# Keeping VectorE's and GpSimd's products apart in the planned order of a fused attention and MLP kernel, and giving GpSimd fewer of them

## The chip, the cores and the metric

The kernel runs on one core of a Trainium2 chip. The metric is the time of one execution on the device in microseconds, less is better. A core has five engines that each work through a fixed list of instructions: TensorE (PE, with its weight loads shown as PEld), VectorE (DVE), ScalarE (ACT), GpSimd (POOL) and SyncE (SP), which issues transfers. They wait for each other by semaphores.

## The reference, cut to what matters

Cosine attention over 8 batches of 12 heads, 448 tokens and 64 columns a head, and then a token-mixing and channel MLP with residuals on what the attention gives.

```
q_n = q / (norm(q) + 1e-6);  k_n = k / (norm(k) + 1e-6)     # unit vectors
attn = softmax(q_n @ k_n.T / tau);  a = attn @ v            # [8, 12, 448, 64]
x = a as [8, 448, 768]
u = x + (x.T @ U @ V).T                                     # U [448, 32], V [32, 448]
out = u + relu(u @ w_ch1) @ w_ch2                           # 768 -> 3072 -> 768
```

## The kernel before

**The work.** Each batch's queries and keys come in three loads of four heads (`load_qk`, L588, issued by GpSimd). For each load `stats` makes the scale of every vector: a square of half a load (`squares`: L636 on ScalarE, L638 on GpSimd or L640 on VectorE), a sum over the head's columns (L644, VectorE), a logarithm and an exponential for the root (L658 and L659, ScalarE), and the inverse (L664 and L666, VectorE). `norm` then makes the unit vectors, for each pair of heads two products with the inverse (L712): part 0 is the queries, part 1 the keys. In batches 0 and 1 the result is transposed by TensorE (L566) and copied by ScalarE or VectorE (L1436, L1438); from batch 2 on SyncE transposes it by a transfer (L728).

The scores of a pair (L774) go to PSUM, ScalarE takes their exponential (L787 and L792), TensorE multiplies by the values (L819), and VectorE divides by the row's sum: L855 and L857 in batches 0 and 1, L850 and L851 later. The division frees the PSUM bank of L819. Token mixing is L934 and L987 on TensorE, and L996 and L998 add its result on VectorE. The MLP works on tiles of 128 tokens of two batches at a time: first three tiles and then one in the plain form (L1372 up, L1414 down, L1425 adds and stores), then twelve pairs of tiles in a Strassen form with seven products instead of eight. The first seven of these use it for the second matrix only (L1260 up, L1289 down), the last five for both (L1153 up). Their sums are L1175, L1232 to L1234, L1243 and L1307 on VectorE and L1314 on GpSimd. `seven_rows` (L1112 to L1115) prepares weights for the last five in buffers that the attention has left.

**The order.** The kernel holds its own planner. Each piece of work is an `Op` with an engine, an assumed duration, what it depends on, what buffers it takes and gives back, and a priority. `Plan.run` plays the work through in assumed time and writes each engine's list in the order in which the play started it. On the chip only this order and the semaphores of the dependencies hold; assumed times do not. TensorE and GpSimd have several streams of work with a fixed order in each; ScalarE, VectorE and SyncE take what is ready by priority. Work that may go to ScalarE or VectorE is decided in the play, too.

An `Op` may be marked `port`. In the play, a marked operation on VectorE does not start while a marked one runs on GpSimd, and the other way round (`shared` in `Plan.run`); nothing on the chip comes from the mark:

```
def shared(o, e, r):
    return max(r, port["POOL" if e == "DVE" else "DVE"]) if o.port and e in port else r
```

The squares and the MLP's weight and sum operations are marked. Of the unit vectors, only those that GpSimd makes are. Which these are stands in `POOL_XN`: part 0 in batches 2 to 7, six products in each batch. GpSimd also makes the four squares of the third load of batch 0. Where the play finds TensorE idle in the first batch, warm-up matmuls (L698) are put in, by the length of the hole.

Of the kernel before, what the change touches and what calls it, by code (L numbers as in the profile page):

```python
# [317 lines left out]
def kernel(  # L318
# [14 lines left out]
    B, H, S, D = q.shape  # L333
# [14 lines left out]
    BURST = [1] + [2] + [3] * 6  # L348
    PLAIN = [3, 1]
    HALF = 7  # L350
    POOL_XN = {x: (0,) for x in range(2, B)}
    WHOLE = 3
    LAST = {0: 0, 2: 2, 4: 4}, {0: 0, 2: 0, 4: 4}
    WIDE = 1
# [69 lines left out]
    class First:  # L424

        slot = uv
# [72 lines left out]
    plan = Plan()  # L499
# [12 lines left out]
    pool_x = plan.stream("POOL")  # L512
# [9 lines left out]
    def dve_t(n, fast=1, fixed=0.065):  # L522
        return fixed + n * 0.00105 / fast

    def any_t(n, fast=1, fixed=0.065):
        return {"ACT": act_t(n), "DVE": dve_t(n, fast, fixed)}
# [27 lines left out]
    def flip(stream, ins, n, into, part, deps, acq, rel, wide=1, eng="ACT/DVE", took=0.05):  # L554


        tp = Slot(r_mm, 1)
        tp.own = True
        for z, x in enumerate(ins):
            def fn(z=z, x=x):  # L560
                if z == 0:
                    w = len(ins) // wide
                    tp.tile = bank_t[:, tp.group[0], :].bitcast(BF)[:, 0:w * n].rearrange(
                        "p (w n) -> p w n", w=w)
                m = 128 // wide
                nc.tensor.transpose(out=tp.tile[m * (z % wide):m * (z % wide + 1), z // wide, :], in_=x(),  # L566
                                    identity=ident[:n, :n])
            o = plan.add(Op("PE", took, fn, deps=deps + [id_set] if z == 0 else (), acq=[tp] + acq,
                            rel=rel if z == len(ins) - 1 else []), stream)
        took = any_t(n * len(ins) // wide, 2)  # L570
        c = plan.add(Op(eng, took, None, deps=[o], acq=acq, rel=[tp], prio=0.2, fast=True))

        def move():
            for dst, src in part(into(), tp.tile):
                copy_op(c, dst, src)
        c.fn = move
        return c
# [45 lines left out]
    def squares(b, g, ld, ops, lo, ii, ss, pr, on, hold, then):  # L623

        red = []
        for i in ii:
            for a0 in range(0, g, G // 2):
                a1 = min(g, a0 + G // 2)
                sq = Slot(r_sq, 1)
                o = Op(on, 1.3 if on == "POOL" else 0.48 if on == "ACT" else 0.44, None,  # L630
                       deps=[ops[i], *hold], acq=[sq], prio=pr + 0.2, fast=True, port=True)

                def square(o=o, i=i, a0=a0, a1=a1, sq=sq):
                    x, y = ld.tile[:, i, lo + a0:lo + a1, :], sq.tile[:, 0:a1 - a0, :]
                    if o.by == "ACT":
                        nc.scalar.activation(out=y, in_=x, func=AF.Square)  # L636
                    elif o.by == "POOL":
                        nc.gpsimd.tensor_mul(y, x, x)  # L638
                    else:
                        nc.vector.tensor_mul(y, x, x)  # L640
                o.fn = square
                plan.add(o, pool_q if on == "POOL" else None)
                red.append(plan.add(Op("DVE", dve_t(256 * (a1 - a0)),
                    lambda i=i, a0=a0, a1=a1, sq=sq: nc.vector.reduce_sum(  # L644
                        ss.tile[:, i, a0:a1, :].rearrange("p h c -> p (h c)"),
                        sq.tile[:, 0:a1 - a0, :].rearrange("p h (c d) -> p (h c) d", d=D),
                        axis=AX.X),
                    deps=[o, *then], acq=[ss], rel=[sq], prio=pr + 0.1)))
        return red
# [50 lines left out]
    def norm(b, p, ld, la, inv, a, deps, pr, loaded):  # L700


        by_pe = b < PE_BATCHES
        first = b == 0 and p == 0
        xn, qkT = Slot(r_xn, 2 if by_pe and (first or (b, p) not in RAW_KEYS) else 1), Slot(r_qkT, SC if b == 0 else sum(p in members(b, x) for x in groups_of(b)))

        def part(i):
            def fn():
                src = ld.tile[:, i, la:la + 2, :].rearrange("p h (c d) -> p h c d", d=D)
                sc = inv.tile[:, i, a:a + 2, :].unsqueeze(3).to_broadcast([SCH, 2, SC, D])  # L710
                dst = xn.tile[:, SC * (1 - i):SC * (2 - i), :].rearrange("p c (h d) -> p h c d", h=2)
                (nc.gpsimd if pool_ else nc.vector).tensor_mul(dst, src, sc)  # L712
            pool_ = i in POOL_XN.get(b, ())
            return plan.add(Op("POOL" if pool_ else "DVE", 1.2 if pool_ else dve_t(512), fn, deps=[deps[i]], acq=[xn],
                               rel=[getattr(ld, "slot", ld), inv], prio=pr, port=pool_), pool_x if pool_ else None)

        def raw():
            c = Op("ACT/DVE", any_t(512), None, deps=loaded[1], acq=[xn], rel=[ld.slot], prio=-0.9)
            c.fn = lambda: copy_op(
                c, xn.tile[:, 0:SC, :].rearrange("p c (h d) -> p h c d", h=2),  # L720
                ld.tile[:, 1, la:la + 2, :].rearrange("p h (c d) -> p h c d", d=D))
            return plan.add(c)

        keys = (b, p) in RAW_KEYS
        ops = {0: part(0), 1: raw()} if first and keys else {0: part(0)} if keys else {
            i: part(i) for i in ((0, 1) if first else (1, 0))}
        if not by_pe:
            done = [plan.add(Op("SP", 0.1, lambda: nc.sync.dma_start_transpose(  # L728
                out=qkT.tile, in_=xn.tile.rearrange("p b e -> p (b e)")), deps=list(ops.values()), acq=[qkT],
                rel=[xn], prio=0, lat=("x", 0.05 * 56, 5.0)))]  # L730
        else:
            done = []
            for i in (1, 0) if keys else ops:
                b0, b1 = SC * (1 - i), SC * (2 - i)
                ins = [(lambda z=z: xn.tile[:, z, :]) for z in range(b0, b1)] if i in ops else [
                    (lambda c=c, hh=hh: ld.tile[:, 1, la + hh, D * c:D * c + D]) for c in range(SC) for hh in range(2)]
                done.append(flip(
                    pe_tp, ins, SCH,
                    lambda: qkT.tile, (lambda t_, x, b0=b0, b1=b1: [(t_[:, b0:b1, :], x)]),
                    [ops[i]] if i in ops else loaded[1], [qkT], [xn if i in ops else ld], len(ins) // SC,  # L740
                    "ACT/DVE", 0.05))
        got[b, p, "qkT"] = (qkT, done, (inv, a, deps[1]))
        return list(ops.values())
# [4 lines left out]
    def members(b, slots):  # L748
        return sorted({p for p, _ in slots} | {p + 1 for p, c in slots if b >= WIDE and c == SC - 1})
# [684 lines left out]
    def copy_op(op, dst, src):  # L1434
        if op.by == "ACT":
            nc.scalar.copy(out=dst, in_=src)  # L1436
        else:
            nc.vector.tensor_copy(out=dst, in_=src)  # L1438
# [52 lines left out]
    def groups_of(b):  # L1491
        if b < WIDE:
            slots = [(p, c) for p in range(NPAIR) for c in range(SC)]
            return [slots[n:n + BURST[b]] for n in range(0, len(slots), BURST[b])]
        slots = []
        for p in range(NPAIR):
            if b >= TB:
                slots += [(x, SC - 1) for x, at in LAST[b > TB].items() if at == p]
            slots += [(p, c) for c in range(SC - 1)] + ([(p - 1, SC - 1)] if p % 2 and b < TB else [])
        return [sorted(slots[n:n + BURST[b]], key=lambda x: x[1] == SC - 1) for n in range(0, len(slots), BURST[b])]  # L1500
# [6 lines left out]
    def att(b):  # L1507
# [18 lines left out]
        acq=[uv], prio=-5, lat=2.5)) for i, src in enumerate((q, k))]  # L1526
# [8 lines left out]
    for c in range(SC):  # L1535
# [8 lines left out]
                        deps=[zf, *begun], prio=-2, lat=12.0))]  # L1544
# [104 lines left out]
```

## Time and profile before

| | |
|---|---|
| median of three runs | 553.93 us (553.42 to 554.13) |
| the profiled execution | 553.89 us, its span 552.1 us |
| TensorE clock granted, mean | 0.997 |
| busy: PE, DVE, ACT, POOL | 542.2, 435.1, 281.4, 184.0 us |
| L712 on DVE, batches 0 to 7 | 58 products, shortest 628 ns, median 682 ns, longest 1532 ns |
| L712 on POOL, batches 2 to 7 | 36 products, shortest 1034 ns, median 1044 ns, longest 1551 ns |
| warm-up matmuls | 142, the last at 31.0 us |
| last exponential of batch 0 ends | 36.86 us |

The profile is of one execution. Busy times of TensorE overlap in its pipeline, so a busy share near 100% does not by itself say that it works at its peak. A line such as L712 can run on two engines and then has two groups. Times within the execution are counted from the start of the span.

### The profile page before, as it was taken

To read this page: it belongs to the slowest core of one execution; us is meant where nothing else is said; L and a number is where in the kernel's file an instruction comes from. 1 tells how busy PE (TensorE), PEld (TensorE's weight loads), DVE (VectorE), ACT (ScalarE), POOL (GpSimd) and SP (SyncE) were. 2 spreads that over 40 slices of the span, in tenths; PEclk is the share of its full clock that TensorE was granted. 3 is DMA by queue.
4 is the path that set the end of the run, shared out by engine and by line. 5 is a ranking of instruction groups with operands and counts; after the bars stand their busy time and mean duration, and the time that the engine had idled before them with its cause. 6 is when DMAs were issued, how large, how long until landed. Compare 5 with 4: busy or idle time off the path is not lost.

```text
span 552.1 us, 14798 instructions
## 1 busy us (share of the span) xinstructions
PE 542.2 (98%) x6085; PEld 390.2 (71%) x6086; DVE 435.1 (79%) x978; ACT 281.4 (51%) x458; POOL 184.0 (33%) x216
## 2 busy tenths in 40 slices
PE   8899999999999999999999999999999999999996
PEld 6565565577857857767767767767778787878784
DVE  8889969989978897798789859657658585858583
ACT  7875746475575656656745754743314141414140
POOL 8626235325533552851543381020101111111111
PEclk9899999999999999999999999999999999999999
DMA  9999999959586949977997494332231312121201
GB/s 147 200 206 144 204 204 148 205 96 139 75 175 108 136 80 172 118 121 160 100 159 135 73 147 102 71 59 60 63 87 31 87 30 87 32 86 30 87 4 57
DMA packets 142324, 61.08 MB, mean 111 GB/s; under 512 B 101008, under 2 KB 142256, under 8 KB 142256
## 3 DMA queue, kind: packets, MB, share of 16 engines
q0 software_dynamic: 72352, 25.73, 43.0%
q1 hardware_dynamic: 69904, 34.41, 29.0%
q8 instruction: 47, 0.77, 0.6%
q14 instruction: 21, 0.17, 0.1%
HBM read 56.93 MB, written 15.93 MB: 132 GB/s over the span
## 4 chain that ended last, share of the span: by engine, by line
PE 91%; DVE 6%; ACT 1%; issue 1%; DMA 1%; DVEq 0%
PE bank L1289 30%; PE bank L1260 20%; PE bank L1153 13%; PE bank L819 8%; PE bank L774 7%; PE bank L1372 6%; PE bank L1414 4%; DVE qk_all L712 2%; PE bank L987 1%; DVE ss L644 1%; ACT attn L787 1%; PE bank L566 1%; PE bank L934 1%; DVE X_sb L857 1%; DMA relu<-in_q_dram 1%
## 5 line engine op out<-in xcount | busy, mean ns | idle before, releaser
L792 ACT ACTIVATE attn<-bank 128x896 bf16<-128x896 f32 (+1 forms) x163 | 140.4, 916 | 44.3 <-PE bank L774 43.8
L1289 PEld LDWEIGHTS <-relu 128*128 128x128 bf16 x1008 | 95.7, 98 | 66.4 <-issue 7.1
L1260 PE MATMUL bank<-uT,w_sb 128*128 128x256 bf16 x1008 | 120.2, 273 | 0.0
L1260 PEld LDWEIGHTS <-w_sb 128*128 128x128 bf16 x1008 | 95.2, 98 | 20.0 <-issue 7.9
L1289 PE MATMUL bank<-w_sb,relu 128*128 128x384 bf16 x576 | 102.7, 326 | 0.0
L712 POOL TENSOR_TENSOR qk_all<-qk_all,inv 112x512 bf16<-112x512 bf16 x36 | 41.0, 1148 | 85.0 <-DMA sqk<-qk_all 39.0
L644 DVE TENSOR_REDUCE ss<-sqk 112x8 f32<-112x512 bf16 x96 | 62.5, 672 | 4.4 <-ACT sqk L636 4.1
L819 PEld LDWEIGHTS <-attn 128*128 128x128 bf16 (+1 forms) x1536 | 55.1, 98 | 7.7 <-issue 4.2
L819 PE MATMUL bank<-v_nat,attn 128*128 128x65 bf16 (+1 forms) x1536 | 58.1, 194 | 0.9 <-DVE X_sb L857 0.4
L1270 ACT ACTIVATE relu<-bank 128x512 bf16<-128x512 f32 x53 | 31.6, 597 | 44.0 <-PE bank L1260 43.8
L774 PE MATMUL bank<-sqk 64*128 64x448 bf16 (+1 forms) x384 | 48.8, 359 | 1.1 <-ACT sqk L1436 0.5
L636 ACT ACTIVATE sqk<-qk_all 112x512 bf16<-112x512 bf16 x56 | 33.8, 632 | 23.3 <-DVE ss L644 22.0
L712 DVE TENSOR_TENSOR qk_all<-qk_all,inv 112x512 bf16<-112x512 bf16 x57 | 45.4, 821 | 0.3
L1153 PEld LDWEIGHTS <-w_sb 128*128 128x128 bf16 x720 | 41.0, 98 | 0.6
L1314 POOL TENSOR_TENSOR relu<-relu,u_nat 128x384 f32<-128x384 f32 x8 | 9.5, 1182 | 91.4 <-ACT relu L1312 91.3
L1190 ACT COPY attn<-bank 128x512 f32<-128x512 f32 x15 | 8.8, 585 | 60.4 <-PE bank L1153 59.5
L611 POOL DMA_DIRECT2D v_nat<-in_v_dram x42 | 31.2, 748 | 15.1 <-DMA w_sb<-in_moe_w_ch_dram 11.8
L1372 PE MATMUL bank<-uT,w_sb 128*128 128x384 bf16 (+1 forms) x288 | 35.6, 273 | 0.0
L1414 PE MATMUL bank<-w_sb,relu 128*128 128x384 bf16 x192 | 35.3, 326 | 0.0
L851 DVE TENSOR_TENSOR X_sb<-bank,rd 128x256 bf16<-128x256 f32 x72 | 30.5, 424 | 2.5
L1307 DVE TENSOR_TENSOR O_sb<-bank,O_sb 128x384 f32<-128x384 f32 x35 | 19.2, 554 | 16.2 <-PE bank L1289 11.5
L1153 PE MATMUL bank<-uT,w_sb 128*128 128x128 bf16 x540 | 31.8, 219 | 0.0
(137 smaller groups left out, 820.0 us busy)
## 6 DMA issues: line engine op xcount, KB each, us to landing
qk_all<-in_q_dram POOLq DMA_DIRECT2D x23, 224.0 KB, 4.4
qk_all<-in_k_dram POOLq DMA_DIRECT2D x23, 224.0 KB, 6.5
u_nat<-u SPq DMA_DIRECT2D x25, 192.0 KB, 2.8
w_sb<-in_moe_w_ch_dram POOLq DMA_DIRECT2D x4, 1152.0 KB, 17.7
w_sb<-in_moe_w_ch_dram POOLq DMA_DIRECT2D x8, 576.0 KB, 15.8
u<-X_sb SPq DMA_DIRECT2D x22, 192.0 KB, 4.7
v_nat<-in_v_dram POOLq DMA_DIRECT2D x11, 168.0 KB, 7.8
out_dram<-O_sb SPq DMA_DIRECT2D x12, 144.0 KB, 2.1
```

Of the source, the lines that this page charges most:

```text
L636: nc.scalar.activation(out=y, in_=x, func=AF.Square)
L644: lambda i=i, a0=a0, a1=a1, sq=sq: nc.vector.reduce_sum(ss.tile[:, i, a0:a1, :].rearrange("p h c -> p (h c)"), sq.tile[:, 0:a1 - a0, :].re ...
L712: (nc.gpsimd if pool_ else nc.vector).tensor_mul(dst, src, sc)
L774: nc.tensor.matmul(out=out, lhsT=qkT.tile.rearrange("p b s -> p (b s)")[r, n0:n0 + w], rhs=qkT.tile[r, SC:2 * SC, :].rearrange("p c s -> p ...
L792: exps.append(plan.add(Op("ACT", act_t(2 * S, 0.08), lambda sc=sc, c=c, attn=attn: nc.scalar.activation(out=attn.tile[:, :, off:off + S] i ...
L819: nc.tensor.matmul(out=av.tile[:, t, 0:D + 1], lhsT=tail.tile[:, hh, 128 * t:128 * (t + 1)] if tail and j == SC - 1 else (attn if j < SC - ...
L1153: o = plan.add(Op("PE", pe_t(128), lambda i=i, j=j, jj=jj: nc.tensor.matmul(out=mm.tile[:, 128 * jj:128 * jj + 128], lhsT=left[k](i, j), r ...
L1260: o = plan.add(Op("PE", pe_t(256), lambda j=j, e=e, cc=cc, mm=mm: nc.tensor.matmul(out=mm.tile[:, 256 * e:256 * e + 256], lhsT=w1_sb[:, cc ...
L1270: nc.scalar.activation(out=dst, in_=mm.tile[:, 0:512], func=AF.Relu)
L1289: o = plan.add(Op("PE", pe_t(CH), lambda j=j: nc.tensor.matmul(out=mm.tile[:, 0:CH], lhsT=left[k](j), rhs=right[k](j), start=(first and j ...
L1372: o = plan.add(Op("PE", pe_t(n), lambda cc=cc: nc.tensor.matmul(out=mm.tile[:, m:m + n], lhsT=w1_sb[:, cc, f * 128:(f + 1) * 128], rhs=uT. ...
L1414: nc.tensor.matmul(out=mm.tile[:, 0:c1 - c0], lhsT=relu.tile[:, f, i * 128:(i + 1) * 128], rhs=w2_t[:, f, c0:c1], start=(f == 0), stop=(f ...
```

## The change

Three things are changed. Unit vectors on VectorE are marked `port` as well, so that the play keeps them apart from every marked operation on GpSimd. GpSimd makes part 0 in batches 2, 3 and 4 only; in 5, 6 and 7 VectorE makes both parts. The durations that the planner assumes for GpSimd are lower: 1.05 us for a unit vector product and 1.02 us for a square.

```
-    POOL_XN = {x: (0,) for x in range(2, B)}
+    POOL_XN = {2:(0,),3:(0,),4:(0,)}
...
-                o = Op(on, 1.3 if on == "POOL" else 0.48 if on == "ACT" else 0.44, None,
+                o = Op(on, 1.02 if on == "POOL" else 0.48 if on == "ACT" else 0.44, None,
                        deps=[ops[i], *hold], acq=[sq], prio=pr + 0.2, fast=True, port=True)
...
             pool_ = i in POOL_XN.get(b, ())
-            return plan.add(Op("POOL" if pool_ else "DVE", 1.2 if pool_ else dve_t(512), fn, deps=[deps[i]], acq=[xn],
-                               rel=[getattr(ld, "slot", ld), inv], prio=pr, port=pool_), pool_x if pool_ else None)
+            return plan.add(Op("POOL" if pool_ else "DVE", 1.05 if pool_ else dve_t(512), fn, deps=[deps[i]], acq=[xn],
+                               rel=[getattr(ld, "slot", ld), inv], prio=pr, port=True), pool_x if pool_ else None)
```

The order changes on every engine, on VectorE from the sums (L644) of batch 0's third load on. In the programs, VectorE has 76 products L712 instead of 58, GpSimd 18 instead of 36, and TensorE 147 warm-up matmuls instead of 142.

## The prediction

> **What bounds the kernel now.** I read the page's first part, then busy time by stretch, then the chain of waits, then the timeline of the one later stretch with a hole in TensorE. First the page's busy shares and, from its fifth part, the groups that the change moves (busy us, mean ns of one, idle time before them).
>
> ```profile
> PE 542.2 (98%) x6085; PEld 390.2 (71%) x6086; DVE 435.1 (79%) x978; ACT 281.4 (51%) x458; POOL 184.0 (33%) x216
> ...
> L712 POOL TENSOR_TENSOR qk_all<-qk_all,inv 112x512 bf16<-112x512 bf16 x36 | 41.0, 1148 | 85.0 <-DMA sqk<-qk_all 39.0
> ...
> L712 DVE TENSOR_TENSOR qk_all<-qk_all,inv 112x512 bf16<-112x512 bf16 x57 | 45.4, 821 | 0.3
> ```
>
> Busy time by stretch: start and end, length, then PE, PEld, DVE, ACT, POOL.
>
> ```profile
> 0.00:40.00 40.00, 35.64 (x472) 25.13 (x473) 33.97 (x99) 32.51 (x58) 24.02 (x35) 0.96 1.30 183
> 40.00:85.00 45.00, 45.00 (x424) 26.68 (x422) 37.90 (x89) 26.09 (x45) 18.83 (x27) 1.00 1.31 184
> 85.00:108.00 23.00, 21.89 (x206) 13.01 (x205) 22.39 (x50) 11.34 (x27) 9.77 (x12) 1.00 1.18 164
> 108.00:210.00 102.00, 101.81 (x1163) 71.85 (x1161) 91.72 (x202) 65.03 (x102) 43.63 (x52) 1.00 0.88 125
> 210.00:380.00 170.00, 170.00 (x1931) 120.73 (x1929) 132.58 (x306) 99.88 (x152) 63.04 (x74) 1.00 0.81 113
> 380.00:548.00 168.00, 167.83 (x1907) 132.79 (x1899) 116.12 (x236) 46.53 (x78) 24.68 (x18) 1.00 0.21 55
> ```
>
> From 108 us on TensorE never rests, and the work ahead of it is the same in both kernels. Time is lost in two places: before 40 us, where batch 0 waits for its exponentials (the 142 warm-up matmuls hide part of that hole), and in 85 to 108, where VectorE is busy 22.4 of 23 us. The chain of waits agrees: 91% TensorE, 6% VectorE, and that 6% lies before 40 and in 89 to 102. The second place, from the timeline:
>
> ```profile
> 88.24 0.35 DVE L666 RECIPROCAL inv<-ln 112x32 f32<-112x32 f32 x1
> ...
> 88.74 2.04 POOL L712 TENSOR_TENSOR qk_all<-qk_all,inv 112x512 bf16<-112x512 bf16 x2 [0.53 <-PE bank L774]
> ...
> 89.82 2.12 DVE L712 TENSOR_TENSOR qk_all<-qk_all,inv 112x512 bf16<-112x512 bf16 x2
> ...
> 91.86 0.17 DVE L855 RECIPROCAL rd<-bank 128x4 f32<-128x4 f32 x1
> ...
> 92.52 0.41 DVE L857 TENSOR_TENSOR X_sb<-bank,rd 128x256 bf16<-128x256 f32 x1
> ...
> 99.21 0.24 PE L934 MATMUL bank<-X_sb,U_sb 128*32 128x128 bf16 x4 [0.70 <-DVE X_sb L857]
> ```
>
> Two L712 on VectorE took 2.12 us where two free ones take 1.26 (2 x 0.63, the shortest in the list of line 712): GpSimd's pair held them up. L855 is then late, L857 gives TensorE its bank back late, and TensorE waits. I count four waits: 0.35 (bank, at 92.6), 0.16, 0.70 (above) and 0.25, together 1.46 us.
>
> Who gets in first, when both are released by one inverse:
>
> ```profile
> 243.19 0.35 DVE L666 RECIPROCAL inv<-ln 112x32 f32<-112x32 f32 x1
> ...
> 243.58 2.14 DVE L712 TENSOR_TENSOR qk_all<-qk_all,inv 112x512 bf16<-112x512 bf16 x2
> 243.62 3.00 POOL L712 TENSOR_TENSOR qk_all<-qk_all,inv 112x512 bf16<-112x512 bf16 x2 [3.27 <-DVE inv L666]
> ```
>
> VectorE's first product ran at once (0.6), GpSimd's first came between (its mate had to wait until about 245.17), then VectorE's second: they alternate. VectorE does not get two in a row, though both stood ready.
>
> **What the Trainium skill says.** "SBUF — State Buffer", section "Who interferes with whom": a VectorE instruction with two SBUF inputs and a GpSimd instruction that reads SBUF exclude each other for a whole instruction, issue order decides who waits, and tensor_reduce does not take part. The trace agrees: 1.53 us for the second product above, while L644 has a mean of 672 ns throughout. "GPSIMD Engine Reference", section "Engine selection", puts two-input elementwise work on GpSimd at about twice VectorE's time; here the medians are 1044 and 682 ns, 1.5 times. "Trainium Kernel Development and Optimization", section "Performance Expectations", calls matmul busy time a bad measure; the 98% above, with warm-ups in it, shows why I go by waits.
>
> **The change part by part.** Nothing in it is a semaphore: it changes what the planner believes, and so the fixed order on each engine. Order views of both programs show the orders quoted below.
>
> (a) *Start, 0 to 40.* The planner now keeps GpSimd's four squares (L638) apart from L712. VectorE's reductions of these squares come earlier: seven L644 stand before the third load's inverse, where there were six. The seventh waits for GpSimd's third square: pair from 12.70, first reduced at 14.5, third square 14.95 to 16.0, reduced at 16.6, then L664 and L666 0.55, an eighth L644 0.63: first L712 at 17.85 instead of 17.17. But before, the first of three was held up by the last square (2.29 for three); now four free ones end at 20.27 against 20.6. ScalarE then does four copies (L1436) in a row and begins its sixteen L792 at 21.3 instead of 20.55, with a Ln/Exp pair (0.5) and a copy (0.45) already behind it. Sixteen at 0.85 (4.23 for five) are 13.6. Before, they ended at 36.86, with waits of 0.52, 0.16 and 0.44 among them. Now I find one wait of about 1.0 (L1480, two L1438 and a memset set stand ahead of the third L855, so TensorE gets its bank at 28.35 and the ninth L792 starts at 29.1) and one of 0.3: end at 36.2. **-0.6**; with no wait -1.9, with a second such wait +0.4. TensorE has no hole in 40 to 85, so this reaches the end. Warm-ups go from 142 to 147; they fill holes and cost nothing.
>
> (b) *85 to 108.* VectorE's order from the second L1425 was L640, L644 x3, L640, L664, L666, L644, L1425, L712 x2, L855, L644, L857. It becomes L644 x4, L664, L666, L640, L712 x2, L1425, L644 x2, L855, L644, L857: both products directly behind the inverse, which also releases GpSimd's two. From 85.29: two L644 to 86.5, Ln and Exp to 87.0, two more L644 to 87.8, L664 and L666 to 88.37 (before 88.59). L640 to 88.75, GpSimd 1.04 to 89.8, L712 0.6 to 90.4, GpSimd to 91.45, L712 to 92.05, L1425 0.5, two L644 1.25, L855 0.2, L644 0.63, L857 0.4: 95.0 instead of 92.93. TensorE, which has one or two L1414 more ahead of it here, comes for the bank at 92.9 and waits 2.1. The second chunk is kept apart as planned: the 0.83 that GpSimd cost L712 at 95.34 goes (1.46 against 0.63), against two more L644; the last L857 ends at 100.6 and L934 waits 0.35. The fourth head waits 0.1. The copy of uT, which was ScalarE's, now stands behind three L712 on VectorE: 0.35. Sum 2.9 against 1.46: **+1.4**. Lower end: VectorE keeps the port, L857 stays at 92.9 and the 0.70 goes, -0.7. Upper end: one more GpSimd product ahead of the uT copy, +2.5. Three queues are touched: SP's transposes (L728) follow L712, and POOL's next L588 follow its products; both feed batch 2, whose first scores come after 105.
>
> (c) *Batches 3 and 4, 108 to 210.* Same six products a batch on GpSimd. The same blocking exists now (1.36 at 140.47) and costs TensorE nothing, because 0.19 us of idle in 102 is all there is. **0**, -0.2 to +0.5.
>
> (d) *Batches 5 to 7.* Eighteen products leave GpSimd and add 18 x 0.68 = 12.3 us to VectorE; blocked time of 2.8 goes (0.71 at 226.19, 0.88 at 243.58 and at 293.17, 0.35 at 340.03). VectorE in 210 to 380 goes from 132.6 to 142.1 of 170, 84%; TensorE has MLP matmuls to fill with. What is hidden stays hidden only where VectorE has gaps; stretches of ten microseconds have it busy 9.50 at 240 and 9.90 at 290. No row shows the cost: at least -0.2, at most +1.5. I take **+0.4**: one wait like that at 92.6 per batch, 0.35 each, less a little. POOL's loads no longer stand behind products there: nothing on the path waits for them.
>
> (e) *End.* After the last L819 the order has 76 L1260 instead of 143, so attention ends 67 x 0.109 = 7.3 us of TensorE work later. From the last L987 to the first L1153 there are 25 x 0.109 + 84 x 0.1625 = 16.4 us (before 24.3). What L1153's first copies need, eight L996 (4.0) and a store's landing (4.7), takes about 9. **0**; if that cover went, up to +0.5.
>
> Planner durations (1.2 to 1.05, 1.3 to 1.02 for GpSimd) move orders only; they are inside the above. Sum: -0.6 + 1.4 + 0.4 = +1.2. The profiled execution took 553.89 (span 552.1 and 1.8 around it), 0.04 under the median 553.93: 555.1.
>
> **Rivals.** *The port is kept (faster).* If VectorE's back-to-back products do hold GpSimd off, (b) is -0.7, (d) 0, (a) -0.6: 552.6. For it: this is what the planner assumes; against it: 243.58. *Even.* GpSimd, which ended its DMA issues at 88.2, is late enough that one product gets between, not two: (b) +0.5, (a) -0.6, (d) 0: 553.8. For it: there is only 0.5 of idle before GpSimd's pair at 88.74. *VectorE becomes the bound in batches 5 to 7 (slower).* It decides where two products more per load fall into the full stretches at 240 and 290: six loads of 1.3 us, of which a third shows, +2.6 instead of +0.4: 557.3. Against it: 37 us of VectorE idle in 210 to 380. That the exclusion is not enforced is no rival but the main case.
>
> **The numbers.** A measurement here tells 0.2%, 1.1 us. Main case 0.40 (554.3 to 556.3), port kept 0.25, even 0.20, VectorE bound 0.15. Slower by over 0.2%: 0.51; within: 0.25; faster: 0.24. Range 552.2 to 557.6: a little past the points of the two outer cases, the port kept (552.6) and VectorE bound (557.3); their own tails, the clean start of (a) at -1.9 and a second blocked chunk in (b), are left out as the 2 in 10.
>
> **What would show it.** The last L792 of batch 0 ends near 36.2, not 36.9. The first L855 behind batch 2's first products starts 2 us after its place before, with a POOL L712 between the two DVE ones; PE's idle in that stretch doubles. DVE has 75 L712 at a mean under 0.75, POOL 18. PE has no hole after 210. It is wrong if L857 there keeps its place against TensorE, or if the loss lies after 210.

## The result, and the profile after

The changed kernel takes 552.62 us (median of 21 executions, 550.99 to 555.00) against 554.10 for the kernel before (21, 553.29 to 555.12) on the same chip. The ratio is 0.9977, with an interval of 0.9968 to 0.9985: **faster by 0.23%**, about 1.4 us. The prediction said 555.1 and slower. The profiled execution took 552.12, with a span of 550.4, 1.7 less than before.

First the page of the changed kernel: busy time of each engine, and the two groups of line 712 (busy us, mean ns of one, idle before them).

```profile
PE 540.6 (98%) x6091; PEld 389.1 (71%) x6091; DVE 444.5 (81%) x996; ACT 281.3 (51%) x458; POOL 163.7 (30%) x198
...
L712 DVE TENSOR_TENSOR qk_all<-qk_all,inv 112x512 bf16<-112x512 bf16 x75 | 53.5, 749 | 1.4 <-DMA sqk<-qk_all 1.1
...
L712 POOL TENSOR_TENSOR qk_all<-qk_all,inv 112x512 bf16<-112x512 bf16 x18 | 19.5, 1092 | 42.9 <-DVE inv L666 22.9
```

Eighteen products went from GpSimd to VectorE, as the code says. Then the changed kernel's busy time by stretch (start and end, length, PE, PEld, DVE, ACT, POOL, then the granted TensorE clock, DMA share and GB/s):

```profile
0.00:40.00 40.00, 34.93 (x483) 24.55 (x484) 33.24 (x99) 33.01 (x61) 23.50 (x34) 1.00 1.30 184
40.00:85.00 45.00, 45.00 (x423) 26.55 (x421) 38.28 (x90) 27.26 (x47) 18.69 (x27) 1.00 1.30 183
85.00:108.00 23.00, 22.98 (x236) 14.38 (x236) 22.21 (x52) 12.19 (x26) 11.47 (x14) 1.00 1.15 173
108.00:210.00 102.00, 102.00 (x1147) 72.39 (x1147) 90.96 (x195) 62.46 (x100) 41.34 (x50) 1.00 0.89 126
210.00:380.00 170.00, 170.00 (x1881) 120.44 (x1880) 141.47 (x323) 100.93 (x152) 43.21 (x56) 1.00 0.88 112
```

TensorE was idle for 1.11 us in 85 to 108 before (23.00 less 21.89); now it is for 0.02. That is the opposite of what part (b) of the prediction said. VectorE is no less busy there. The timeline of the changed kernel shows why (start, length, instruction, count; VectorE first, then GpSimd, then TensorE):

```profile
84.22 2.45 DVE L644 TENSOR_REDUCE ss<-sqk 112x8 f32<-112x512 bf16 x4
86.59 0.18 DVE L664 TENSOR_SCALAR ln<-ln 112x32 f32<-112x32 f32 x1
86.81 0.35 DVE L666 RECIPROCAL inv<-ln 112x32 f32<-112x32 f32 x1
...
87.36 1.28 DVE L712 TENSOR_TENSOR qk_all<-qk_all,inv 112x512 bf16<-112x512 bf16 x2
...
90.97 0.42 DVE L857 TENSOR_TENSOR X_sb<-bank,rd 128x256 bf16<-128x256 f32 x1
...
87.50 1.24 POOL L616 DMA_DIRECT2D v_nat<-in_v_dram  x2 [0.71 <-DMA v_nat<-in_v_dram]
88.76 2.06 POOL L712 TENSOR_TENSOR qk_all<-qk_all,inv 112x512 bf16<-112x512 bf16 x2
...
92.05 0.65 PE L819 MATMUL bank<-v_nat,attn 128*128 128x65 bf16 x16
```

The inverse is done at 87.16. GpSimd is still issuing value loads (L616) and begins its products at 88.76, about 0.1 us after VectorE's second product has ended (88.64). So the pair on VectorE takes 1.28 us, not 2.12, L857 gives the bank back at 91.4, and TensorE takes it at 92.05 without a wait. A margin of 0.1 us between two engines that nothing ties together made me suspect that other executions fall on the other side. The 21 times fit that: 12 lie at 552.81 or below, 9 at 553.43 or above, and none between. The granted clock does not divide them: it is 0.998 to 1.000 in both groups.

### The profile page after: what moved, and what is told of

Read it like the earlier page. It is cut to its first block, busy times and chain, and to the rows that moved or that the text cites. A ratio compares the mean times of both kernels' runs of the same rounds, so it can differ in the third digit from the quotient of the medians.

```text
span 550.4 us, 14785 instructions
## 1 busy us (share of the span) xinstructions
PE 540.6 (98%) x6091; PEld 389.1 (71%) x6091; DVE 444.5 (81%) x996; ACT 281.3 (51%) x458; POOL 163.7 (30%) x198
## 4 chain that ended last, share of the span: by engine, by line
PE 94%; DVE 4%; DMA 1%; POOL 1%; issue 0%; ACT 0%; DVEq 0%; POOLq 0%
PE bank L1289 30%; PE bank L1260 20%; PE bank L1153 13%; PE bank L819 8%; PE bank L774 7%; PE bank L1372 6%; PE bank L1414 6%; PE bank L987 2%; DVE qk_all L712 1%; PE bank L934 1%; DVE ss L644 1%; DMA relu<-in_q_dram 1%; POOL sqk L638 1%; PE bank L566 1%; DVE X_sb L857 0%; DVE sqk L1438 0%
## 5 line engine op out<-in xcount | busy, mean ns | idle before, releaser
L792 ACT ACTIVATE attn<-bank 128x896 bf16<-128x896 f32 (+1 forms) x163 | 139.2, 915 | 46.2 <-PE bank L774 45.9
L644 DVE TENSOR_REDUCE ss<-sqk 112x8 f32<-112x512 bf16 x96 | 62.5, 674 | 2.4 <-ACT sqk L636 1.9
L712 DVE TENSOR_TENSOR qk_all<-qk_all,inv 112x512 bf16<-112x512 bf16 x75 | 53.5, 749 | 1.4 <-DMA sqk<-qk_all 1.1
L1270 ACT ACTIVATE relu<-bank 128x512 bf16<-128x512 f32 x50 | 29.9, 598 | 39.0 <-PE bank L1260 38.8
L774 PE MATMUL bank<-sqk 64*128 64x448 bf16 (+1 forms) x384 | 48.3, 357 | 1.0 <-ACT sqk L1436 0.6
L1314 POOL TENSOR_TENSOR relu<-relu,u_nat 128x384 f32<-128x384 f32 x8 | 9.9, 1236 | 102.0 <-ACT relu L1312 102.0
L588 POOL DMA_DIRECT2D qk_all<-in_q_dram x24 | 17.7, 738 | 74.1 <-issue 29.8
L1272 DVE TENSOR_SCALAR relu<-bank 128x512 bf16<-128x512 f32 x34 | 23.3, 687 | 12.5 <-PE bank L1260 11.3
L712 POOL TENSOR_TENSOR qk_all<-qk_all,inv 112x512 bf16<-112x512 bf16 x18 | 19.5, 1092 | 42.9 <-DVE inv L666 22.9
```

What stands on the lines that cost most here:

```text
L644: lambda i=i, a0=a0, a1=a1, sq=sq: nc.vector.reduce_sum(ss.tile[:, i, a0:a1, :].rearrange("p h c -> p (h c)"), sq.tile[:, 0:a1 - a0, :].re ...
L774: nc.tensor.matmul(out=out, lhsT=qkT.tile.rearrange("p b s -> p (b s)")[r, n0:n0 + w], rhs=qkT.tile[r, SC:2 * SC, :].rearrange("p c s -> p ...
L792: exps.append(plan.add(Op("ACT", act_t(2 * S, 0.08), lambda sc=sc, c=c, attn=attn: nc.scalar.activation(out=attn.tile[:, :, off:off + S] i ...
```

## The experiments

**Theory A**: what counts is whether a GpSimd product holds up a VectorE instruction that TensorE waits for, and that is decided anew in each execution by small shifts of time. **Rival B**: fewer products on GpSimd bring the gain. **C**: the separation brings it. **D**: VectorE pays for its eighteen products. **E**: the separation makes VectorE wait where it could have worked. **F**: the order of the instructions is what differs, whatever GpSimd does. In the first four expectations, A still stands for less: that the square's price alone brings the new start and the closed hole. All times are medians, with the ratio to the kernel before on the same chip (whose medians are 553.9 to 554.4); the chip changes from one group of runs to the next.

### One part of the change at a time

Only the square's assumed duration (`sq_price`):

```
-                o = Op(on, 1.3 if on == "POOL" else 0.48 if on == "ACT" else 0.44, None,
+                o = Op(on, 1.02 if on == "POOL" else 0.48 if on == "ACT" else 0.44, None,
```

> The kernel before with one number of the change: GpSimd's square (L638) is priced at 1.02 instead of 1.3. Its order in 0 to 108 us is the changed kernel's up to the fourth head of batch 1, though no product is kept apart that was not before; after that it is an order of its own. Theory A (the gain of the changed kernel is the new order of the start, about -0.9, and the closed hole of 85 to 108, about -1.0, and both come from this one price): 552.1 to 552.9, ratio 0.996 to 0.998, inverse of batch 2 near 87 us with two DVE L712 right behind it, and a last L792 of batch 0 near 36.0. Rival B (GpSimd's fewer products in batches 5 to 7 bring it): 554.1, ratio 1.000. Rival C (keeping VectorE's products and GpSimd's apart brings it): 554.1 or a little under, with the second products still held up.

Measured 557.73 (555.95 to 559.88), ratio 1.0057 (1.004 to 1.0075): slower, against everything I had expected. Its profiled execution took 559.88. VectorE and GpSimd in it, where the instructions up to L857 are the same as in the changed kernel:

```profile
87.57 0.35 DVE L666 RECIPROCAL inv<-ln 112x32 f32<-112x32 f32 x1
87.84 0.36 DVE L640 TENSOR_TENSOR sqk<-qk_all 112x512 bf16<-112x512 bf16 x1
88.12 3.55 DVE L712 TENSOR_TENSOR qk_all<-qk_all,inv 112x512 bf16<-112x512 bf16 x2
...
89.05 2.06 POOL L712 TENSOR_TENSOR qk_all<-qk_all,inv 112x512 bf16<-112x512 bf16 x2
...
94.36 0.65 PE L819 MATMUL bank<-v_nat,attn 128*128 128x65 bf16 x16 [1.37 <-DVE X_sb L857]
```

VectorE is 0.76 us later than in the changed kernel's profile (its k load and with it a transpose came late near 8 us), GpSimd 0.29. That is enough: the pair takes 3.55 us, and TensorE waits 1.37 here and 0.75 for a later L857. The hole of the prediction is real; it had not opened in the other profile.

The changed kernel without its `POOL_XN` line (`no_xn`; 36 products stay on GpSimd):

```
-    POOL_XN = {2:(0,),3:(0,),4:(0,)}
+    POOL_XN = {x: (0,) for x in range(2, B)}
```

> The changed kernel without one part: GpSimd keeps its products in batches 5 to 7 (36 in all). TensorE's order is instruction for instruction the changed kernel's. Theory A (the eighteen products cost or bring nothing where they run): within 0.2% of the changed kernel, 552.3 to 553.1. Rival B (fewer GpSimd products, so less blocking of VectorE, bring the gain): 554.1. Rival D (VectorE pays for the eighteen products, 12.3 us more of its time in 210 to 380): faster than the changed kernel by 0.4 to 1.5, 551.1 to 552.2.

Measured 551.15, ratio 0.9954 (0.9939 to 0.997). Six executions: four from 550.93 to 551.19, two at 553.10 and 553.33. B falls: the gain does not need fewer products. D seems to hold, but two groups of times so far apart make a median of six a poor measure; the runs with copies below price it better. The expectation calls TensorE's order the changed kernel's own; in the traces the two part at 229 us. The same holds for the next run and the kernel before, from 221 us on.

The `POOL_XN` line alone (`xn_alone`):

```
-    POOL_XN = {x: (0,) for x in range(2, B)}
+    POOL_XN = {2:(0,),3:(0,),4:(0,)}
```

> The kernel before with one part of the change: GpSimd makes products in batches 2 to 4 only (18 instead of 36). TensorE's order is the same as before, instruction for instruction. Theory A: no difference, 553.9 to 554.5. Rival B (less blocking on VectorE is the gain): 552.6. Rival D (VectorE has no room for eighteen more products): 554.5 to 555.6.

Measured 554.74, ratio 1.0007 (0.9999 to 1.0016): no gain. B falls again. The time is in D's range, but the interval does not tell it from no change.

The separation alone (`port_alone`):

```
-                               rel=[getattr(ld, "slot", ld), inv], prio=pr, port=pool_), pool_x if pool_ else None)
+                               rel=[getattr(ld, "slot", ld), inv], prio=pr, port=True), pool_x if pool_ else None)
```

> The kernel before with one part of the change: the planner keeps VectorE's products (L712) and GpSimd's apart; prices and POOL's share as before. Theory A (the start's order is almost the old one here, so no gain there; only what the hole of 85 to 108 happens to do): 553.4 to 554.4, ratio 0.9985 to 1.0005. Rival C (the separation itself is the gain): 552.6, ratio 0.9975, with DVE's L712 at a mean under 0.75 us. Rival E (the separation makes VectorE wait where it could have worked): 555 or more.

Measured 559.25, ratio 1.009 (1.0077 to 1.0103): the slowest of all. C falls. E named 555 or more; the fills below decide on it. Its TensorE idles 2.91 us in 108 to 210 and 2.05 in 210 to 380, where the kernel before has 0.19 and none. One of these places, VectorE, then GpSimd, then TensorE:

```profile
231.03 2.72 DVE L1233 TENSOR_TENSOR relu<-relu 128x384 bf16<-128x384 bf16 x1
...
231.46 2.06 POOL L712 TENSOR_TENSOR qk_all<-qk_all,inv 112x512 bf16<-112x512 bf16 x2
...
234.67 0.38 PE L1260 MATMUL bank<-uT,w_sb 128*128 128x256 bf16 x2 [1.71 <-DVE relu L1272]
```

L1233, a sum of the MLP that takes 0.34 us where it is free, takes 2.72 beside two GpSimd products; L1272 behind it is late, and TensorE waits 1.71. Here both operations had always been marked, so the planner meant to keep them apart. Its assumed times and the chip's had drifted.

### Is it GpSimd's reading, or the order?

In the next two, and in two later ones, every product on GpSimd is replaced by a fill of the same target. "SBUF — State Buffer" in the Trainium skill, section "Who interferes with whom", says that a VectorE instruction with two SBUF inputs contends with a GpSimd instruction that reads SBUF, not with one that only writes it. The order of the instructions stays. What these kernels leave out is GpSimd's unit vectors, so their output is not the attention of the reference.

```
+ pool_ and nc.gpsimd.tensor_copy(out=peek, in_=inv.tile[0:1, i, a, 0:1])   # waits for the same inverse
- (nc.gpsimd if pool_ else nc.vector).tensor_mul(dst, src, sc)
+ nc.gpsimd.memset(dst, 0.0) if pool_ else nc.vector.tensor_mul(dst, src, sc)
```

> The kernel with the square's price alone (557.7), but each of GpSimd's 36 products is replaced by filling its target with a constant, behind a copy of one element of the same inverse: GpSimd is busy at the same places, but reads no second operand out of SBUF (the output is not the attention of the reference; the order on every engine is the same). Theory A (GpSimd's products hold up VectorE instructions that TensorE waits for): the waits of 2.1 in 85 to 108, 3.1 in 108 to 210 and 0.8 at 434 shrink to under 1.5 in all, 551 to 553. Rival F (the order of the instructions itself is worse, whatever GpSimd does): 557 or more, with the same waits.

> The kernel with the separation alone (559.3), with the same replacement of GpSimd's 36 products by a fill (the output is not the attention of the reference). Theory A: VectorE's L1233 near 231 takes 0.34 instead of 2.72, TensorE's waits for L1272 (2.6) go, 552 to 555; the wait of 1.16 for L1404 at 119.9, where no GpSimd product runs, stays. Rival F: 558.5 or more.

`sq_free` takes 551.40 (0.995; 0.9938 to 0.9963), 6.3 less than with the products. `port_free` takes 551.74 (0.9959; 0.9946 to 0.9971), 7.5 less. Busy time by stretch, first of the kernel with the square's price alone, then of the same with fills:

```profile
85.00:108.00 23.00, 20.88 (x195) 12.36 (x194) 22.80 (x47) 10.93 (x25) 11.23 (x14) 1.00 1.18 167
108.00:210.00 102.00, 98.92 (x1145) 70.83 (x1143) 89.33 (x196) 60.37 (x94) 44.65 (x51) 1.00 0.87 117
```

```profile
85.00:108.00 23.00, 23.00 (x237) 14.40 (x237) 22.14 (x53) 12.79 (x27) 9.03 (x20) 1.00 1.44 193
108.00:210.00 102.00, 102.00 (x1150) 72.36 (x1149) 85.91 (x201) 61.61 (x97) 37.31 (x65) 1.00 0.93 129
```

5.2 us of TensorE's idle time (2.12 and 3.08) are gone. F falls, and E with it: three orders that lie 6.7 us apart with GpSimd's products (552.6, 557.7 and 559.3) lie within 0.7 without them (551.08, see below, 551.40 and 551.74). A fill is shorter than a product (0.51 against 1.04), so this takes some of GpSimd's load away too; the copies below do not. I had also expected the wait for L1404 near 120 in `port_alone` to stay, since no product runs there. It went too, so it came from earlier blocking; by what path is not shown.

The same for the kernel before (`before_free`):

> The kernel before with GpSimd's 36 products replaced by a fill (the output is not the attention of the reference; the order on every engine is the same). It splits the gain of the change. If the new start is worth 1.1 by itself and the rest is blocking: the hole of 1.46 in 85 to 108 shrinks to under 0.4, the start stays, time 552.2 to 553.0. If blocking is all and the start is made up for later: 551.2 to 551.9. If blocking costs the kernel before nothing: 554.1.

552.33 (0.9966; 0.9953 to 0.998). Blocking costs the kernel before 1.8 us. What then still divides it from the changed order without blocking (`after_free` below) is 1.2 by the times and 0.9 by the ratios. In the two profiles it is 0.8: the start 0.5 and waits of TensorE 0.35.

### Who is ready first in 85 to 108

GpSimd brought forward (`after_early`): in the changed kernel, the last four value loads of batch 2 are issued behind the first two products.

```
-    ops.append(load(lambda e=e, hh=hh, c=c, s0=s0, s1=s1: nc.gpsimd.dma_start(
+    ops.append(load(lambda e=e, hh=hh, c=c, s0=s0, s1=s1: (later_v_.append if b == 2 else lambda f: f())(lambda: nc.gpsimd.dma_start(
...
+    n_xn_[:2] == [2, 2] and later_v_ and [f() for f in [later_v_.pop(0) for _ in later_v_[:]]]   # behind GpSimd's second product
```

> The changed kernel, with one difference on GpSimd's queue alone: batch 2's first two products go ahead of that batch's last four value loads (L616), not behind them. They then wait for the inverse and nothing else, as the prediction assumed. Theory A (the changed kernel escapes the predicted hole only because GpSimd is still issuing loads when VectorE's two products run): VectorE's pair behind the inverse takes 2.1 to 3.6 us instead of 1.28, TensorE waits 1.5 to 2.5 in 85 to 108, time 554 to 555.5, ratio to before 1.000 to 1.002. Rival (VectorE keeps the port for back-to-back products whoever is ready): pair 1.3 us, no hole, 552.6.

```profile
86.41 0.35 DVE L666 RECIPROCAL inv<-ln 112x32 f32<-112x32 f32 x1
...
86.96 2.99 DVE L712 TENSOR_TENSOR qk_all<-qk_all,inv 112x512 bf16<-112x512 bf16 x2
...
86.91 2.49 POOL L712 TENSOR_TENSOR qk_all<-qk_all,inv 112x512 bf16<-112x512 bf16 x2 [3.13 <-DVE inv L666]
```

When both stand ready they alternate, as at 243.58 in the kernel before: the pair takes 2.99. VectorE does not keep the port. But the time is only 552.89 (0.9979; 0.997 to 0.9988), with 11 executions within 552.34 to 553.56: TensorE waits 0.82 once, since the inverse is so early (86.4) that L857 still comes at 92.2. My expectation of 554 to 555.5 was too high, because it charged the blocking and forgot the slack.

GpSimd held back (`after_guard`): a copy of one element of VectorE's latest product ahead of each product on GpSimd.

```
+ on GpSimd, ahead of the product:   nc.gpsimd.tensor_copy(out=peek, in_=latest[-1])
+ on VectorE, with each product:     latest.append(dst[0:1, 0, 0, 0:1])
```

> The changed kernel with a copy of one element ahead of each of GpSimd's products, from the tile that VectorE's latest product wrote: GpSimd then can't begin before that product is done, on any execution. Theory A (in some executions of the changed kernel GpSimd gets in first, and those are its long ones of 554 to 555): median 551.2 to 552.4, longest under 553.5. Rival (the spread comes from elsewhere, such as the landing of the first loads): 552.6 with single executions up to 555 as before.

551.39 (0.9947; 0.9934 to 0.9959), executions from 550.63 to 551.68: none lies at 553.4 to 555. Five are few, but the two other kernels with copies below have none there either, 15 executions in all. Of the 1.2 under the changed kernel, 0.4 is the end of the program (part (e) below).

The changed kernel once more (`after_again`):

> The changed kernel once more, for a second profiled execution and more times. If its long executions (554 to 555) are those in which VectorE comes later to batch 2's first products than GpSimd, a profile of such an execution shows VectorE's pair behind the inverse of batch 2 at 2.1 to 3.6 us and a TensorE wait of 0.8 to 2 in 85 to 108; a short one (551 to 552.5) shows 1.28 and no wait. Times again spread over 551 to 555.

552.56 (0.9976; 0.9966 to 0.9986), and again in two groups. Over both series 26 of 43 executions lie within 550.99 to 552.81 (median 552.2) and 17 within 553.43 to 555.00 (median 554.1). The profiled one, 552.03, was of the first group, with a pair of 1.28.

VectorE made late by three more inverses (`after_late`, and with the copies `after_late_guard`; the four take 1.51 us, one takes 0.35), and the changed order without blocking (`after_free`):

```
-            nc.vector.reciprocal(inv.tile[:, w, 0:g, :], nv.tile[:, w, 0:g, :])
+            for _ in range(4 if (b, h0) == (2, 0) else 1): nc.vector.reciprocal(inv.tile[:, w, 0:g, :], nv.tile[:, w, 0:g, :])
```

> The changed kernel with one delay: VectorE makes the inverse of batch 2's first load (L666) four times over instead of once, so its two products come 0.85 us later, while GpSimd's queue stays as it is. Theory A (the side on which this meeting falls sets the long executions): VectorE's pair takes 2.1 to 3.6 us instead of 1.28, TensorE waits 1.5 to 3 in 85 to 108, and nearly every execution is long: median 553.8 to 555, none under 553. Rival G (a delay of VectorE costs what it is and no more, long executions come from elsewhere): 552.6 to 553.4, with some executions still under 552.5.

> The same delay of 0.85 us on VectorE, with the copy of one element ahead of each of GpSimd's products, so that they stay behind VectorE's. Theory A: the pair takes 1.28 us again, TensorE waits 0.2 to 0.7, median 551.4 to 552.2: the delay alone is cheap, the meeting is dear. Rival G: the same time as without the copies.

> The changed kernel with GpSimd's 18 products replaced by a fill (the output is not the attention of the reference). Theory A: no long executions, 551.0 to 551.6, as with the copies of one element. If batches 5 to 7 pay for their eighteen products on VectorE, it stays above the square's price without blocking (551.4) by 0.3 or more.

`after_late`: 555.47 (1.0027; 1.001 to 1.0045), seven of nine executions at 554.95 or more, two at 552.96 and 553.00. The median is above A's range, and A had expected no short ones. `after_late_guard`: 551.86 (0.9962; 0.995 to 0.9975). The delay by itself costs 0.5 (551.86 less 551.39); the meeting with GpSimd makes it 2.9 (555.47 less 552.56). Six of the seven long executions also have a lower granted clock, 0.995 to 0.997 against 0.998 and 1.000 in the short ones, so part of the 2.9 can be the clock. `after_free`: 551.08 (0.995; 0.9937 to 0.9962). Rival G falls. D does not show either: without blocking the changed order is not above the square's price alone (551.40). One of the 13 executions of the kernel before beside these took 550.83, 2 us under the next of 85; why is not known.

The profile of `after_late` was one of its two short executions: GpSimd came at 89.73, after VectorE's pair. Even there TensorE waits 1.15 at 98.6, behind a product that took 1.91 at 94.25. A second profile:

> The changed kernel with VectorE delayed by 0.85 us ahead of batch 2's first products, for one more profile. If it is a long execution (555 to 556): GpSimd's first product begins within 0.6 us after VectorE's first, VectorE's pair takes 2.1 to 3.6 us, TensorE waits 1.5 to 3 in 85 to 108. If it is a short one (under 553.5): pair 1.28 and GpSimd's first product later than VectorE's second. A long execution with a pair of 1.28 would refute theory A.

554.94, a long one. VectorE, GpSimd and TensorE in it:

```profile
88.20 0.36 DVE L640 TENSOR_TENSOR sqk<-qk_all 112x512 bf16<-112x512 bf16 x1
88.48 2.99 DVE L712 TENSOR_TENSOR qk_all<-qk_all,inv 112x512 bf16<-112x512 bf16 x2
...
88.43 2.49 POOL L712 TENSOR_TENSOR qk_all<-qk_all,inv 112x512 bf16<-112x512 bf16 x2 [0.66 <-PE bank L1414]
...
94.17 0.65 PE L819 MATMUL bank<-v_nat,attn 128*128 128x65 bf16 x16 [1.98 <-DVE X_sb L857]
```

This is the prediction's part (b) nearly number for number: products from 88.5 (GpSimd's first from 88.75 predicted), GpSimd's between them, TensorE waiting 1.98 (2.1 predicted). That the whole time agrees, 554.9 against 555.1, is in part luck: it has the delay in it, and the kernel before took 554.29 on that chip. By its times, the changed kernel is not there in most executions.

### Better versions

All products on VectorE (`none_on_pool`), and the two best edits together (`no_xn_guard`, which is `no_xn` with the copies of `after_guard`):

```
-    POOL_XN = {2:(0,),3:(0,),4:(0,)}
+    POOL_XN = {}
```

> The changed kernel with no product on GpSimd at all: 93 L712 on VectorE, none on POOL, in an order of its own. It has nothing that blocks but the four squares of the start, and 12.3 us more of VectorE's time in batches 2 to 4. If blocking is the only loss there is, 551 to 552. If VectorE has no room for the products in 85 to 210 (22.2 of 23 us busy in 85 to 108), 553 to 556, with TensorE waits in 85 to 210 for L857 or the copies.

> The changed kernel with GpSimd's 36 products kept and with the copy of one element ahead of each: the two best edits so far together. Expected 550.6 to 551.4, no single execution over 552.5. If the copies hold GpSimd's products up so far in batches 5 to 7 that the transposes for the next scores come late, 551.5 to 553 with TensorE waits after 210.

`none_on_pool`: 552.96 (0.9974; 0.9967 to 0.9982), within 552.21 to 553.44. I was wrong that nothing else blocks. In its profile, VectorE and GpSimd:

```profile
270.17 3.44 DVE L640 TENSOR_TENSOR sqk<-qk_all 112x512 bf16<-112x512 bf16 x2
273.54 0.54 DVE L1307 TENSOR_TENSOR relu<-bank,relu 128x384 f32<-128x384 f32 x1
...
270.33 0.92 POOL L1314 TENSOR_TENSOR relu<-relu,u_nat 128x384 f32<-128x384 f32 x1
271.21 1.78 POOL L1314 TENSOR_TENSOR O_sb<-relu,u_nat 128x384 f32<-128x384 f32 x2
```

Three of GpSimd's MLP sums (L1314) hold up the first of two squares, which takes 3.11 us; the second takes 0.41. L1307 is late, and TensorE waits 1.02 at 274.

`no_xn_guard`: 551.18 (0.994; 0.9927 to 0.9954), 550.52 to 551.34: 3.0 under the kernel before and 1.4 under the changed one (552.56) on the same chip, of which 0.4 is the end of the program (part (e) below). It is the fastest of those that compute the reference, with no gap to `after_guard` that these few executions could show; `no_xn` has the same median (551.15) but long executions too.

## Why the prediction was right or wrong

**What bounds the kernel**: right. TensorE without holes is the limit; with GpSimd's products replaced by fills, every order lands at 551.1 to 552.3.

**(a) Start, -0.6: right in sign, too small, and TensorE's clock was overlooked.** ScalarE's first L1402, behind batch 0's exponentials and the first MLP matmuls, starts at 42.57, 43.00 and 42.15 with the old order (before, `xn_alone`, `before_free`; mean 42.57) and at 40.90 to 42.35 with the new one (thirteen profiles, mean 41.55): -1.0. Before and after:

```profile
42.57 0.87 ACT L1402 ACTIVATE relu<-bank 128x384 bf16<-128x384 f32 x2 [1.31 <-PE bank L1372]
41.58 0.87 ACT L1402 ACTIVATE relu<-bank 128x384 bf16<-128x384 f32 x2 [1.31 <-PE bank L1372]
```

The mis-sized term is the wait ahead of the ninth L792, put at 1.0; it is 0.35, and the one put at 0.3 is 0.18. Batch 0's last exponential ends at 35.9, not 36.2, in spite of a first load that landed 0.6 later in that execution. The separation alone has an early start as well (41.50 and 40.92 with fills).

The prediction took the kernel before's wait of 0.52 at 23.17 for a matter of its order. The granted clock says more. The stretch from 20.6 to 24 us, first before, then after:

```profile
20.60:24.00 3.40, 3.35 (x42) 2.39 (x40) 2.48 (x8) 2.84 (x5) 2.84 (x4) 0.50 1.16 210
20.60:24.00 3.40, 2.64 (x40) 1.65 (x39) 3.37 (x9) 3.39 (x6) 2.25 (x3) 1.00 1.16 210
```

TensorE had half its clock there before, and an L774 took 0.55 us instead of 0.36; ScalarE's wait of 0.52 is for such an L774. All three profiles of the old order have a stretch of 3.4 us like this, from 20.6, 20.3 and 18.9; none of the fifteen others has one ahead of its last matmul. So the gain of the start is the new order together with a clock that does not fall, and no edit parts the two. An estimate of the clock's share: of 85 executions of the kernel before, the 14 with a mean clock of 0.998 or more have a median of 553.9, the others 554.3, so about 0.4 of the 1.0.

**(b) 85 to 108, +1.4: this step turned the sign.** The instructions were read rightly, and so was the alternation; what failed is the walk "From 85.29". That is VectorE's time in the kernel before. The gain of (a) brings VectorE there 1.07 earlier (four L644 from 84.22), and the inverse is done at 87.16, not 88.37. GpSimd is not moved along: its loads wait for other transfers, its queue was free at 88.2 before and at 88.74 now, and its first product begins at 88.76 where the walk had 88.75. So GpSimd's place in the walk was right and VectorE's was 1.2 late: I left out of (b) what I had credited in (a). L857 ends at 91.39 instead of 95.0: 1.2 by the earlier inverse, 2.1 because no GpSimd product runs between, 0.3 by steps that overlap. That is also the prediction's own sign of being wrong, that L857 keeps its place against TensorE. (The 1.46 that it counts as waits before is 1.10 of idle time in the trace: 0.10, 0.16, 0.70 and 0.14.) The rival "even" named the right mechanism, a GpSimd that is late, and stopped half way, at one product between. "The port is kept" named the right time, 552.6, for a wrong reason, as `after_early` shows: luck.

**And it is not one number.** In the profiles of all orders that have this pair on VectorE behind the same inverse, GpSimd's queue came free from 87.8 to 89.7. VectorE's first product begins between 87.0 and 88.1 in those without an added delay, its second 0.6 later. So the two can meet on either side, and the changed kernel's times lie at 552.2 or 554.1. That GpSimd's products make the long group is shown by its absence with the copies and the fills, which act on all eighteen products. That it is this meeting rests on `after_late`, which moves VectorE from here on, and on one profile of each side (pair 2.99 long, 1.28 short). There is no profile of the unaltered changed kernel in the long group, so for it the cause stays likely, not shown. The causes of the shifts (landing of first loads, pace of GpSimd's issues) are seen, but not what sets them.

**What the gain is made of.** In the two profiles the span is 1.74 shorter. L1402 starts 0.99 earlier, TensorE idles 1.28 less after it (1.30 before, 0.02 after), the end below takes 0.43 more, and 0.1 is left over. By the medians, blocking costs the changed kernel 1.1 (552.6 less 551.1, less 0.4 for the end, which `after_free` does not have), against 1.8 in the kernel before. So the start gives about 1, less blocking about 0.7, and the end takes 0.4 back. The medians come from different chips; these parts are good to some tenths.

**(c) Batches 3 and 4, 0: right for this order**, for TensorE idles not at all in 108 to 210. But `sq_price` and `port_alone` lose 3 us there, so "costs TensorE nothing" was no property of the stage.

**(d) Batches 5 to 7, +0.4: not refuted, not told from 0.** VectorE's 141.5 us in 210 to 380 was forecast as 142.1. With the copies on both sides, the eighteen products cost 0.2 (551.39 against 551.18); `xn_alone` makes it 0.4 (-0.1 to +0.9), with blocking in it; `after_free` shows no cost. VectorE is not the bound there; that rival falls.

**(e) End, 0: right for TensorE, 0.4 missed behind it.** TensorE has no hole from 380 to its last matmul. But here are the last stores' issues, before and after, in spans of 552.1 and 550.4:

```profile
548.45 0.78 SPq L1057 DMA_DIRECT2D out_dram<-O_sb  x2
546.28 0.78 SPq L1057 DMA_DIRECT2D out_dram<-O_sb  x2
```

From there to the end of the span it takes 2.87 us before and 3.30 after. The long end stands in all five profiles of the changed kernel and its two edits of timing (`after_early`, `after_late`), 2.9 in all thirteen others, those with copies and `no_xn` among them. So 0.4 of what those two gain over the changed kernel is this end and not blocking. What makes it is not known.

## What to carry to other kernels

When one step of a change moves an engine in time, move it in all later steps, and ask which engines move with it and which are paced by something else: a meeting of two engines is decided by their difference. Where a shared resource is kept free only by a planned order, plan and chip drift apart; three orders of the same work differed by 6.7 us, nearly all of it through this, and one-element copies that make the later engine wait brought the planned order back for about 0.2 us of GpSimd each. Look at all times before explaining a median: two groups with a gap can be two courses of one program. And add the parts of a measured gain up to the whole, clock and end included: here the end took 0.4 us that no step of the prediction had.

## What the runs showed of the hardware that I had not expected

- A blocked VectorE instruction can lose two or three GpSimd instructions in a row, not one. Started together with them, they alternate (2.99 for two of each, twice). But L1233 took 2.72, and the second product of `sq_price` 2.95, beside two GpSimd products that by the records began 0.4 and 0.3 us after it, and a square of `none_on_pool` 3.11 beside three sums of 0.92, the first 0.16 after it. The skill's section cited above has issue order decide; by these records the later one went first. Starts on GpSimd are rough in the profile, so which is at fault stays open.
- A fill on GpSimd did not hold VectorE up: in `port_free` the pair takes 1.28 us from 88.22, with GpSimd's fills at 88.23 and 88.88. This agrees with that section. Nor did GpSimd's issuing of transfers (87.50 to 88.74 in the changed kernel, pair 1.28).
